# Two PSUM drains moved behind a branch, and earlier transposes of w3 with fewer load slots, in a one-core attention and mixture-of-experts kernel

## The chip, the cores and the metric

The kernel runs on one core of one Trainium2 chip. The metric is the device time of one launch in microseconds: the span from the first to the last instruction on the engines, and the little that lies around it. Three timed runs of the kernel before gave 1210.71, 1212.91 and 1214.0 us; their median is 1212.91 us. One more execution was taken with the profiler, and all rows below come from it.

## What is computed

Attention with a softmax over the features of q and over the sequence of k, then a mixture of eight experts with top-1 routing, then a bilinear network whose last two matrices follow each other without anything between them:

```python
def _moe_ref(x, modality_id, w_gate, modality_bias, w1, w2):
    ...
    for e in range(E):
        mask = e_idx == e
        h = np.maximum(x[mask] @ w1[e], 0.0)
        out[mask] = gate_w[mask, None] * (h @ w2[e])

def _moe2_ref(x, w1, w2, w3, w_out):
    a = x @ w1
    b = x @ w2
    h = a * b @ w3
    return h @ w_out
```

There are 4608 tokens of 512 features, 8 experts with 1024 hidden features, and in the last network w3 of 1024 by 1024 and w_out of 1024 by 512. All is float32 and stays that exact: an operand is split into a rounded part (hi) and the rest (lo), and each product is three matmuls (hi by hi, hi by lo, lo by hi).

## The kernel before

Attention comes first. Then the tokens, sorted by expert, go through ten **slots**: nine of 512 tokens and one of 256. A slot (the function `slot`, in parts that its argument names) loads the expert's W1 and W2 and gathers its tokens (part "l"), splits W1 on ScalarE and VectorE and transposes the tokens on TensorE (part "s"), multiplies by W1 in eight pieces m = 0 to 7 of 128 hidden features (part "a"; L752), each drained by a ReLU on ScalarE (L756) and a subtraction on VectorE (L757), and multiplies by W2 in four pieces (part "b"; L772), each drained by ScalarE (L775). The eight pieces of the W1 product take turns in PSUM banks 0, 1 and 2; the W2 product uses banks 3 and 4, the transposes of the tokens (L735) banks 5 and 7.

How many slots the experts need is known on the chip only. Behind part "a" of the **fourth slot** (n = D0 = 3) every engine loads the number `need` (L895), compares it and branches (L896). The body of the branch, with further slots, is for unlucky routings and does not run here. At the join each engine waits for its own semaphore and then adds to it what the body would have added, so that waits behind the join hold on both ways. Part "b" of the fourth slot stands behind the join.

After the slots comes a **stage of preparation** for the last network. w3 and w_out depend on no token, so they are multiplied with each other first, in eight blocks fb: `turned` loads 128 rows of w3, transposes them on TensorE into banks 5 and 7 (L978, four transposes for each half z) and splits each half on ScalarE (L966, out of PSUM) and VectorE (L967); `product` multiplies a block by the split w_out (L991, twelve matmuls for a half) into bank 3 or 4, which ScalarE drains (L994). In the same stage `factors` makes the operands of the last multiplication, a scheme of seven products in place of eight: four blocks, each of two loads, four sums on GpSimd (L1016) and seven splits on ScalarE (L1024) and VectorE (L1025). That multiplication (`quarter`, L1098) follows as soon as its token operands, loaded by `positions` (L1071), are split.

The loads of w_out, w3 and of the two factor matrices (their names in the rows are wo_f, w_f and m_f) go through five slots of 1024 floats in the tile `ca`, taken in turn (`ring`, `stage`; L959 and L961). The transposed and split halves of w3 live in four places (`th`): two for even blocks in `al` and `thm`, two for odd blocks in `tt`, which takes the place of the W2 product's output tile `yo`.

The order of all this on each engine is set by a planner (class `Plan`): every step has an engine, a cost, the keys that it reads and writes, and a rank, which is its place in the program plus `pri`; among the steps that can start, an engine takes the one of lowest rank. There is one plan ahead of the branch and one behind it. Semaphores are then set from the memory that instructions touch.

Of the kernel before, what the change touches and what calls it, by code (L numbers as in the profile page):

```python
# [142 lines left out]
def body(tc, q, k, v, mod, wgate, mbias, w1, w2, m1, m2, w3, wo, out):  # L143
# [529 lines left out]
    def slot(P, n, after=(), parts="lsab", T=None, again=False):  # L673
# [47 lines left out]
        if "s" in parts:  # L721
# [3 lines left out]
            for h in hs:  # L725
                for kp in range(2):
# [13 lines left out]
                    P.add("V", vt_(512), lambda hi=hi, lo=lo, p=p: V.tensor_tensor(lo(), p, hi().bitcast(F32), op=ALU.subtract), r=[K("bk", pb), K("xh", h, kp)], w=[K("xl", h, kp, "t")] + ([K("opened")] if n == 0 else []), pri=-230)  # L740

        if "a" in parts:
            for m in range(8):
                pb = m % 3
                p = lambda pb=pb: bank[pb][:, 0:N]
                ms = slice(128 * m, 128 * m + 128)

                for kk in range(4):

                    def mm(p=p, ms=ms, kk=kk):  # L750
                        for c, (i, z) in enumerate(PAIRS):
                            PE.matmul(p(), lhsT=W1(i)[:, TURN[kk], ms], rhs=XT(z)[:, kk, cols], start=(kk == 0 and c == 0), stop=(kk == 3 and c == 2))  # L752

                    P.add("P", 3 * one, mm, r=[K(x, TURN[kk] + 4 * (m // 4)) for x in ("w1h", "w1l")] + [K("xh", h, kk // 2) for h in hs] + [K("xl", h, kk // 2, "t") for h in hs] + ["Mb"], w=[K("bk", pb)])
                hh, hl = (lambda m=m: HT(0)[:, m, cols]), (lambda m=m: HT(1)[:, m, cols])
                P.add("S", ps_(N), lambda hh=hh, p=p: SC.activation(hh(), p(), AF.Relu), r=[K("bk", pb), "Mb"], w=[K("hh", h, m) for h in hs])  # L756
                P.add("V", vt_(N), lambda hh=hh, hl=hl, p=p: V.scalar_tensor_tensor(out=hl(), in0=p(), scalar=0.0, in1=hh().bitcast(F32), op0=ALU.max, op1=ALU.subtract),  # L757
                      r=[K("bk", pb)] + [K("hh", h, m) for h in hs], w=[K("hl", h, m) for h in hs])
            for f in range(8):
                split("w2", f, lambda f=f: M["w2r"][:, f], lambda f=f: W2(0)[:, f], lambda f=f: W2(1)[:, f], "Mb")  # L760

        if "b" in parts:
# [144 lines left out]
    for n in range(D0, X0):  # L907
        if n < D0 + 2:
            slot(P, n, parts="b" if n == D0 else "sab", T=aheads[n - D0])
        else:  # L910
            slot(P, n)
        units += 2 if n < F0 else 1
        while done < nj and done < NJ + (nj - NJ) * units // (2 * ND + NF - 1):
            doubles(done, *jobs[done])
            done += 1
# [25 lines left out]
    old = [K(x, i) for x in ("w1h", "w1l", "w2h", "w2l") for i in range(8)] + [K(x, b, i) for x in ("hh", "hl") for b in range(2) for i in range(8)]  # L941
    old += [K("xh", b, i) for b in range(2) for i in range(2)] + [K("xl", b, i, "t") for b in range(2) for i in range(2)]
    hand_over(old, two("Mf", 4))
    hand_over([K(x, i) for x in ("st", "T", "Q", "O") for i in range(2)] + [K("xg", b, i) for b in range(2) for i in range(2)], two("ring", 5) + two("tmp", 4) + two("ev", 2))
# [5 lines left out]
    def th(i, q, g=0, n=4):  # L950
        t, a = (("al", 8192), ("thm", 0), ("tt", 0), ("tt", 1024))[q]
        a += 512 * i + 128 * g
        return flat(M[t][:, a : a + 128 * n], n)

    def stage(nm, r):

        t, kk = ring[rot("ring", 5)]
        if nm == "wo":
# [4 lines left out]

    def split(src, sk, hi, lo, hk, lk, n, psum=False):

        P.add("S", (ps_ if psum else sb_)(n), lambda: SC.copy(hi(), src), r=sk, w=[hk])  # L966
        P.add("V", vt_(n), lambda: V.tensor_tensor(lo(), src, hi().bitcast(F32), op=ALU.subtract), r=list(sk) + [hk], w=[lk])  # L967

    def turned(fb):
        t, kk = stage("w3", fb)  # L970
        p2 = fb % 2
        for z in range(2):
# [6 lines left out]

            P.add("P", 0.43, tr, r=kk, w=[K("bk", pb)])  # L980
            q = 2 * p2 + z
            split(flat(bank[pb], 4), [K("bk", pb)], lambda q=q: th(0, q), lambda q=q: th(1, q), K("th", q), K("tl", q), 512, True)

    def product(fb):
        p2, pb = fb % 2, 3 + fb % 2
        for z in range(2):

            def mm(z=z):
                for g in range(4):
                    for n, (i, y) in enumerate(PAIRS):  # L990
                        PE.matmul(bank[pb], lhsT=th(i, 2 * p2 + z, g, 1)[:, 0], rhs=WO(y, 4 * z + g), start=(z == 0 and g == 0 and n == 0), stop=(z == 1 and g == 3 and n == 2))  # L991

            P.add("P", 2.73, mm, r=[K(x, 2 * p2 + z) for x in ("th", "tl")] + [K(x, g) for g in range(4 * z, 4 * z + 4) for x in ("wo", "wol")], w=[K("bk", pb)])
        P.add("S", ps_(512), lambda: SC.copy(evict[p2], bank[pb]), r=[K("bk", pb)], w=[K("ev", p2)])  # L994
# [32 lines left out]
    for r in range(4):  # L1027
        t, kk = stage("wo", r)
        for g in range(2):
            z = 2 * r + g  # L1030
            split(t[:, 512 * g : 512 * g + 512], kk, lambda z=z: WO(0, z), lambda z=z: WO(1, z), K("wo", z), K("wol", z), 512)
    turned(0)
    for fb in range(8):
        if fb < 7:
            turned(fb + 1)
        product(fb)
        if fb < 4:
            factors(fb // 2, fb % 2)


    t, kk = ring[rot("ring", 5)]
    oraw, orow = t[0:36, 0:256], t[0:36, 512:640]
# [243 lines left out]
```

## Time and profile before

| what | us |
|---|---|
| median of three timed runs | 1212.91 |
| the profiled execution, its own time | 1208.95 |
| its span, first to last instruction | 1207.2 |
| TensorE (PE) busy | 1130.9 |
| VectorE (DVE) busy | 859.3 |
| GpSimd (POOL) busy | 538.7 |
| ScalarE (ACT) busy | 526.3 |

The profiled execution lies 3.96 us below the median of the timed runs, and 1.75 us of its time lie outside the span. TensorE is the busiest engine by far, so the profile is read for what ends its idle times. A busy share says how long an engine had an instruction, not that it ran at its peak; the clock that TensorE was granted has a column of its own. PEld is TensorE's loading of weights, which overlaps its matmuls; a name with q (PEldq, DVEq) is an engine's instruction queue, where waits, loads of registers and branches stand.

### The profile page before, as it was taken

What the parts mean: (1) busy time and instruction counts of PE and PEld (TensorE: products, weight loads), DVE (VectorE), ACT (ScalarE), POOL (GpSimd) and SP (SyncE); (2) the same over time, 40 slices, a digit from 0 to 9 for tenths busy, and PEclk for the clock granted to TensorE, in tenths of its full rate; (3) what the DMA queues carried; (4) which work ended last, traced back from release to release, by engine and by line L of the source; (5) the groups of instructions that cost most, each with busy time, mean ns of one, the idle gap of its engine ahead of it and who ended that gap; (6) DMA issues with size and microseconds to landing.
All of it is one profiled execution on the core that took longest, in us unless ns stands there. A gap on an engine that the chain in (4) does not pass through costs nothing.

```text
span 1207.2 us, 22895 instructions
## 1 busy us (share of the span) xinstructions
PE 1130.9 (94%) x8605; PEld 1029.5 (85%) x8605; DVE 859.3 (71%) x1441; ACT 526.3 (44%) x1003; POOL 538.7 (45%) x538
## 2 busy tenths in 40 slices
PE   4777889999899999999999999999999999999996
PEld 3566768788788888888977999999999999999995
DVE  7979887997577787877594766656575689765550
ACT  3546455345344534533563232424232445655550
POOL 0445248853233333342260556454555576443332
PEclk9868789999999999999999999999999999999998
DMA  9982577773276467373673343434343438987741
GB/s 354 390 315 92 162 207 169 147 284 118 90 226 182 128 210 210 102 245 138 212 225 109 105 122 118 138 103 137 117 120 118 127 104 279 345 250 234 236 141 47
DMA packets 156140, 216.00 MB, mean 179 GB/s; under 512 B 19791, under 2 KB 90995, under 8 KB 156019
## 3 DMA queue, kind: packets, MB, share of 16 engines
q1 hardware_dynamic: 148946, 195.00, 50.8%
q0 software_dynamic: 7072, 19.44, 5.6%
q8 instruction: 69, 1.13, 0.4%
q14 instruction: 53, 0.43, 0.1%
HBM read 156.35 MB, written 74.82 MB: 191 GB/s over the span
## 4 chain that ended last, share of the span: by engine, by line
PE 67%; DVE 3%; issue 1%; DMA 1%; ACT 0%; POOL 0%; SPq 0%; DVEq 0%; POOLq 0%; ACTq 0%
PE pb L1098 29%; PE pb L1231 13%; PE pb L772 12%; PE pb L752 10%; PE pb L991 2%; DVE ar L1025 2%; PE pb L735 1%; DMA ca<-p_dram 0%; DMA p_dram<-ca 0%; DVE ar L967 0%; PE pb L978 0%; POOL out_dram L1205 0%; DVE tt L967 0%; DVE al L967 0%; DVE ca L1121 0%
## 5 line engine op out<-in xcount | busy, mean ns | idle before, releaser
L1098 PE MATMUL pb<-al,ar 128*128 128x384 f32 x1728 | 308.5, 336 | 1.1 <-ACT sx L1104 0.8
L1098 PEld LDWEIGHTS pb<-al,ar 128*128 128x128 f32 x1728 | 301.1, 188 | 1.6 <-ACT sx L1104 1.1
L772 PE MATMUL pb<-ar 128*128 128x512 f32 (+1 forms) x960 | 213.8, 381 | 0.0
L752 PE MATMUL pb<-ar 128*128 128x512 f32 (+1 forms) x960 | 212.5, 381 | 0.2 <-DVE ar L757 0.2
L752 PEld LDWEIGHTS pb<-ar 128*128 128x128 f32 x960 | 173.9, 189 | 34.3 <-DVE ar L757 0.6
L772 PEld LDWEIGHTS pb<-ar 128*128 128x128 f32 x960 | 173.2, 189 | 33.0
L1231 PE MATMUL pb<-ar 128*128 128x256 f32 x1512 | 182.8, 283 | 2.2 <-ACT ar L966 1.1
L1231 PEld LDWEIGHTS pb<-ar 128*128 128x128 f32 x1512 | 181.8, 192 | 3.2 <-ACT ar L966 1.3
L967 DVE TENSOR_TENSOR ar<-ca,ar 128x512 fp32r<-128x512 f32 x140 | 107.4, 776 | 54.6 <-ACT ar L966 52.7
L966 ACT CAST ar<-ca 128x512 fp32r<-128x512 f32 x140 | 86.0, 622 | 46.9 <-DMA ca<-p_dram 14.5
L756 ACT ACTIVATE ar<-pb 128x512 fp32r<-128x512 f32 (+1 forms) x80 | 46.2, 578 | 112.0 <-PE pb L752 111.9
L802 POOL TENSOR_TENSOR ca<-ca 128x512 f32<-128x512 f32 x40 | 56.4, 1415 | 79.9 <-DVE ca L801 72.1
L1104 ACT COPY sx<-pb 128x384 f32<-128x384 f32 x96 | 46.1, 482 | 90.5 <-PE pb L1098 63.9
L757 DVE SCALAR_TENSOR_TENSOR ar<-pb,ar 128x512 fp32r<-128x512 f32 (+1 forms) x80 | 52.7, 659 | 37.9 <-ACT ar L756 37.8
L330 POOL TENSOR_TENSOR kt<-kt,kr 128x384 f32<-128x384 f32 x36 | 45.2, 1294 | 75.0 <-ACT kr L324 60.0
L1132 POOL TENSOR_TENSOR ca<-ca 128x384 f32<-128x384 f32 x48 | 53.5, 1114 | 46.9 <-DVE ca L1132 46.9
L1107 POOL TENSOR_TENSOR ca<-ca,sx 128x384 f32<-128x384 f32 x24 | 27.3, 1139 | 95.3 <-ACT sx L1104 95.3
L775 ACT COPY yo<-pb 128x512 f32<-128x512 f32 (+1 forms) x40 | 22.6, 566 | 107.2 <-PE pb L772 97.3
L688 DVE TENSOR_TENSOR ar<-w2r,ar 128x512 fp32r<-128x512 f32 x60 | 46.2, 796 | 28.0 <-ACT ar L686 27.0
L1104 ACT COPY ca<-pb 128x384 f32<-128x384 f32 x48 | 23.0, 481 | 87.1 <-PE pb L1098 82.3
L688 POOL TENSOR_TENSOR ar<-w2r,ar 128x512 fp32r<-128x512 f32 x20 | 28.2, 1411 | 69.2 <-ACT ar L686 69.1
L1098 PE MATMUL pb<-thm,ar 128*128 128x384 f32 x288 | 59.0, 340 | 0.0
(282 smaller groups left out, 1781.3 us busy)
## 6 DMA issues: line engine op xcount, KB each, us to landing
p_dram<-ca SPq DMA_DIRECT2D x168, 192.0 KB, 2.3
ca<-p_dram SPq DMA_DIRECT2D x126, 256.0 KB, 3.8
w1r<-in_moe_w_dram SPq DMA_DIRECT2D x10, 2048.0 KB, 7.8
w2r<-in_moe_w_dram SPq DMA_DIRECT2D x10, 2048.0 KB, 9.5
ca<-in_moe_w_dram SPq DMA_DIRECT2D x32, 512.0 KB, 4.1
kt<-in_k_dram SPq DMA_DIRECT2D x8, 1152.0 KB, 10.8
qt<-in_q_dram SPq DMA_DIRECT2D x8, 1152.0 KB, 13.2
vt<-in_v_dram SPq DMA_DIRECT2D x8, 1152.0 KB, 16.2
```

What stands on the lines that cost most here:

```text
L688: P.add(g, c, lambda: e.tensor_tensor(lo(), raw(), hi().bitcast(F32), op=ALU.subtract), r=[K(nm + "r", i), K(nm + "h", i), extra], w=[K(nm ...
L752: PE.matmul(p(), lhsT=W1(i)[:, TURN[kk], ms], rhs=XT(z)[:, kk, cols], start=(kk == 0 and c == 0), stop=(kk == 3 and c == 2))
L756: P.add("S", ps_(N), lambda hh=hh, p=p: SC.activation(hh(), p(), AF.Relu), r=[K("bk", pb), "Mb"], w=[K("hh", h, m) for h in hs])
L757: P.add("V", vt_(N), lambda hh=hh, hl=hl, p=p: V.scalar_tensor_tensor(out=hl(), in0=p(), scalar=0.0, in1=hh().bitcast(F32), op0=ALU.max, o ...
L772: PE.matmul(p(), lhsT=W2(i)[:, f, ns], rhs=HT(y)[:, f, cols], start=(f == 0 and c == 0), stop=(f == 7 and c == 2))
L802: P.add("G", gt_(512), lambda: G.tensor_tensor(Tf, Tf, Qf, op=ALU.add), r=[K("Q", b)], w=[K("T", b)])
L966: P.add("S", (ps_ if psum else sb_)(n), lambda: SC.copy(hi(), src), r=sk, w=[hk])
L967: P.add("V", vt_(n), lambda: V.tensor_tensor(lo(), src, hi().bitcast(F32), op=ALU.subtract), r=list(sk) + [hk], w=[lk])
L1098: PE.matmul(bk(j), lhsT=Mt[:, f, a, i, m, t], rhs=X(y, x)[:, t], start=(fresh and t == 0 and n == 0), stop=(t == 1 and n == 2), skip_group ...
L1104: P.add("S", ps_(HB), lambda j=j, to=to: SC.copy(S(to), bk(j)), r=[bkk(j)], w=[sk(to)])
L1132: P.add(eng, c(HB), lambda: e.tensor_tensor(t[:, sl], x, y, op=op), r=kk, w=[k_])
L1231: PE.matmul(bk(j), lhsT=At[z][:, m, i, f], rhs=Bt[:, x, y, f], start=(fresh and f == 0 and n == 0), stop=(f == 3 and n == 2), skip_group_c ...
```

## The change

Three things are edited. First, the drains of pieces 6 and 7 of the fourth slot's W1 product (a ReLU and a subtraction each) are taken out of part "a", which stands ahead of the branch, into a part "z" that the plan behind the branch begins with. The matmuls stay where they are. Second, the loads of w3 get two slots of the ring for themselves, and w_out and the factors the other three. Third, the transposes of w3 and their splits get a lower rank (`pri` of -120, and -400 for block 0), and block 1 puts its two halves into `ar`, into memory that the W1 halves of the slots held and that the factors of the second matrix take later.

```diff
+        def leave(m):
+            pb = m % 3
+            p = lambda pb=pb: bank[pb][:, 0:N]
+            hh, hl = (lambda m=m: HT(0)[:, m, cols]), (lambda m=m: HT(1)[:, m, cols])
+            P.add("S", ps_(N), lambda hh=hh, p=p: SC.activation(hh(), p(), AF.Relu), r=[K("bk", pb), "Mb"], w=[K("hh", h, m) for h in hs])
+            P.add("V", vt_(N), lambda hh=hh, hl=hl, p=p: V.scalar_tensor_tensor(out=hl(), in0=p(), scalar=0.0, in1=hh().bitcast(F32), op0=ALU.max, op1=ALU.subtract),
+                  r=[K("bk", pb)] + [K("hh", h, m) for h in hs], w=[K("hl", h, m) for h in hs])
...
+                if n != D0 or m < 6:
+                    leave(m)
...
+        if "z" in parts:
+            for m in (6, 7):
+                leave(m)
...
-            slot(P, n, parts="b" if n == D0 else "sab", T=aheads[n - D0])
+            slot(P, n, parts="zb" if n == D0 else "sab", T=aheads[n - D0])
...
+    hand_over(old[:16], [K(x, i) for x in ("th", "tl") for i in (4, 5)])
...
-        t, a = (("al", 8192), ("thm", 0), ("tt", 0), ("tt", 1024))[q]
+        t, a = (("al", 8192), ("thm", 0), ("tt", 0), ("tt", 1024), ("ar", 3584), ("ar", 4608))[q]
...
-        t, kk = ring[rot("ring", 5)]
+        t, kk = ring[3 + rot("w3", 2) if nm == "w3" else rot("ring", 3)]
...
+    quarter_of = lambda fb, z: 4 + z if fb == 1 else 2 * (fb % 2) + z
+
-    def turned(fb):
+    def turned(fb, ahead=-120):
...
-            P.add("P", 0.43, tr, r=kk, w=[K("bk", pb)])
-            q = 2 * p2 + z
-            split(flat(bank[pb], 4), [K("bk", pb)], lambda q=q: th(0, q), lambda q=q: th(1, q), K("th", q), K("tl", q), 512, True)
+            P.add("P", 0.43, tr, r=kk, w=[K("bk", pb)], pri=ahead)
+            q = quarter_of(fb, z)
+            split(flat(bank[pb], 4), [K("bk", pb)], lambda q=q: th(0, q), lambda q=q: th(1, q), K("th", q), K("tl", q), 512, True, ahead)
...
-    turned(0)
+    turned(0, -400)
...
+        if fb == 1:
+            hand_over([K(x, i) for x in ("th", "tl") for i in (4, 5)] + two("Mf", 4), [])
```

Where it moves instructions is shown by the order of the two built programs. VectorE before the change, the last rows ahead of the branch (L757 is a subtraction; pb_2296, pb_2297 and pb_2298 are banks 0, 1 and 2):

```order
L757 SCALAR_TENSOR_TENSOR ar<-pb_2298,ar 128x512
L757 SCALAR_TENSOR_TENSOR ar<-pb_2296,ar 128x512
L757 SCALAR_TENSOR_TENSOR ar<-pb_2297,ar 128x512
L757 SCALAR_TENSOR_TENSOR ar<-pb_2298,ar 128x512
L757 SCALAR_TENSOR_TENSOR ar<-pb_2296,ar 128x512
L757 SCALAR_TENSOR_TENSOR ar<-pb_2297,ar 128x512
L895 TENSOR_LOAD need
L896 COMPARE_AND_BRANCH
```

VectorE with the change, the first rows behind the join (L747 is the same subtraction, L740 the split of the transposed tokens out of banks 5 and 7):

```order
L906 UNCONDITIONAL_BRANCH x2
L747 SCALAR_TENSOR_TENSOR ar<-pb_2296,ar 128x512
L747 SCALAR_TENSOR_TENSOR ar<-pb_2297,ar 128x512
L740 TENSOR_TENSOR ar<-pb_76,ar 128x2x256
L740 TENSOR_TENSOR ar<-pb_78,ar 128x2x256
L688 TENSOR_TENSOR ar<-w1r,ar 128x512 x3
```

The two last subtractions of the fourth slot stand behind the join instead of ahead of the branch; ScalarE's two ReLUs moved in the same way. TensorE before the change, from the last slot's W2 product (L772) into the stage of preparation (L978 transposes, L991 products):

```order
L772 MATMUL pb_2299<-ar 128x256 x24
L772 MATMUL pb_75<-ar 128x256 x24
L772 MATMUL pb_2299<-ar 128x256 x24
L772 MATMUL pb_75<-ar 128x256 x24
L978 MATMUL pb_76<-ident,ca 128x128 x4
L978 MATMUL pb_78<-ident,ca 128x128 x4
L978 MATMUL pb_76<-ident,ca 128x128 x4
L991 MATMUL pb_2299<-al 128x512 x12
L978 MATMUL pb_78<-ident,ca 128x128 x4
L991 MATMUL pb_2299<-al,thm 128x512 x12
```

TensorE with the change, the same place (L782 is the W2 product, L991 are now the transposes):

```order
L782 MATMUL pb_2299<-ar 128x256 x12
L991 MATMUL pb_76<-ident,ca 128x128 x4
L991 MATMUL pb_78<-ident,ca 128x128 x4
L782 MATMUL pb_2299<-ar 128x256 x12
L782 MATMUL pb_75<-ar 128x256 x3
L991 MATMUL pb_76<-ident,ca 128x128 x4
L782 MATMUL pb_75<-ar 128x256 x3
L991 MATMUL pb_78<-ident,ca 128x128 x4
L782 MATMUL pb_75<-ar 128x256 x18
L991 MATMUL pb_76<-ident,ca 128x128 x4
L991 MATMUL pb_78<-ident,ca 128x128 x4
L782 MATMUL pb_2299<-ar 128x256 x24
```

The transposes of blocks 0, 1 and 2 stand among the matmuls of the last W2 product; behind it, products come at once.

## Rows read from the trace of the kernel before

**Rows 1.** The chain that ended last: start us, length us, what.
```profile
328.92 3.41 PE pb L772 x12
332.32 0.87 PE pb L735 x8
333.20 19.09 PE pb L772 x84
...
589.69 11.53 PE pb L772 x96
...
657.18 1.05 PE pb L1098 x6
```

**Rows 2.** Stretches: length, busy PE, PEld, DVE, ACT, POOL, PEclk, DMA share, GB/s.
```profile
326.90:330.10 3.20, 3.12 (x12) 2.86 (x13) 2.38 (x4) 2.83 (x6) 0.00 (x0) 0.50 0.19 5
330.20:333.60 3.40, 3.40 (x20) 2.88 (x20) 2.92 (x5) 2.26 (x5) 1.36 (x1) 1.00 0.07 1
```

**Rows 3.** Timeline around the branch: start us, length us, engine, line, what [idle before].
```profile
317.37 0.60 ACT L756 ACTIVATE ar<-pb 128x512 fp32r<-128x512 f32 x1 [2.40 <-PE pb L752]
318.00 0.69 DVE L757 SCALAR_TENSOR_TENSOR ar<-pb,ar 128x512 fp32r<-128x512 f32 x1 [2.31 <-ACT ar L756]
322.47 0.60 ACT L756 ACTIVATE ar<-pb 128x512 fp32r<-128x512 f32 x1 [2.06 <-PE pb L752]
323.10 0.69 DVE L757 SCALAR_TENSOR_TENSOR ar<-pb,ar 128x512 fp32r<-128x512 f32 x1 [1.96 <-ACT ar L756]
326.98 1.94 PE L735 MATMUL pb<-ident,ca 128*128 128x128 f32 x8 [4.54 <-DVEq L896]
```

**Rows 4.** Line 896, the branch: durations (ns min/median/max), first and last start us.
```profile
L896 PEldq COMPARE_BRANCH  x1: 3732/3732/3732, 318.8 to 318.8; - x1
L896 PEldq EVENT_SEMAPHORE  x1: 51/51/51, 322.6 to 322.6; - x1
L896 ACTq EVENT_SEMAPHORE  x1: 17/17/17, 325.9 to 325.9; - x1
L896 DVEq EVENT_SEMAPHORE  x1: 21/21/21, 326.8 to 326.8; - x1
```

**Rows 5.** The columns of rows 2: the last W2 product, then the stage of preparation.
```profile
589.70:601.20 11.50, 11.50 (x98) 11.50 (x98) 3.13 (x6) 3.53 (x8) 3.92 (x4) 1.00 0.62 217
601.20:657.00 55.80, 52.28 (x257) 42.39 (x255) 38.07 (x46) 28.73 (x53) 20.03 (x13) 1.00 0.55 175
```

**Rows 6.** TensorE's waits from 601.3 to 657 us: total, times, longest.
```profile
PE pb L978 <- DVE al L967: 1.5, 1, 1.5
PE pb L978 <- DVE tt L967: 1.0, 1, 1.0
PE pb L991 <- DVE al L967: 1.0, 1, 1.0
```

**Rows 7.** ScalarE's timeline, splits of w_out during the last slot.
```profile
590.20 0.62 ACT L966 CAST al<-ca 128x512 fp32r<-128x512 f32 x1 [1.01 <-DMA ca<-wo_f]
...
591.00 1.65 ACT L966 CAST al<-ca 128x512 fp32r<-128x512 f32 x3
```

**Rows 8.** Lines 1025 and 967 by form: durations (ns min/median/max), first and last start.
```profile
L1025 DVE TENSOR_TENSOR ar<-ca,ar x28: 676/681/1790, 602.2 to 637.0; 128x512 fp32r<-128x512 f32 x28
L967 DVE TENSOR_TENSOR tt<-pb,tt x8: 674/680/692, 606.7 to 647.0; 128x512 fp32r<-128x512 f32 x8
```

**Rows 9.** Timeline of GpSimd and VectorE, second and last block of factors.
```profile
611.23 5.94 POOL L1016 TENSOR_TENSOR ca<-ca 128x512 f32<-128x512 f32 x4 [8.88 <-DMA ca<-m_f]
...
632.57 5.07 DVE L1025 TENSOR_TENSOR ar<-ca,ar 128x512 fp32r<-128x512 f32 x7
```

**Rows 10.** Lines 961 and 1071, loads: time from issue to landing.
```profile
DMA to landing us min/median/max: 4.1/4.9/9.4
DMA to landing us min/median/max: 3.7/4.7/5.6
```

**Rows 11.** Groups of instructions from 601.2 to 657 us: busy us, mean ns | idle before.
```profile
L1025 DVE TENSOR_TENSOR ar<-ca,ar 128x512 fp32r<-128x512 f32 x28 | 27.6, 1036 | 8.2 <-ACT ar L1024 8.2
```

More of the change, by code (lines that the diff above doesn't have):

```diff
@@ L754, in slot @@
                     P.add("P", 3 * one, mm, r=[K(x, TURN[kk] + 4 * (m // 4)) for x in ("w1h", "w1l")] + [K("xh", h, kk // 2) for h in hs] + [K("xl", h, kk // 2, "t") for h in hs] + ["Mb"], w=[K("bk", pb)])
[L755 to L758, printed above, removed]
+                if n != D0 or m < 6:
+                    leave(m)
             for f in range(8):
                 split("w2", f, lambda f=f: M["w2r"][:, f], lambda f=f: W2(0)[:, f], lambda f=f: W2(1)[:, f], "Mb")
+        if "z" in parts:
+            for m in (6, 7):
+                leave(m)
         if "b" in parts:
@@ L962, in stage, with split @@
         return t, kk
-    def split(src, sk, hi, lo, hk, lk, n, psum=False):
-        P.add("S", (ps_ if psum else sb_)(n), lambda: SC.copy(hi(), src), r=sk, w=[hk])
-        P.add("V", vt_(n), lambda: V.tensor_tensor(lo(), src, hi().bitcast(F32), op=ALU.subtract), r=list(sk) + [hk], w=[lk])
-    def turned(fb):
+    def split(src, sk, hi, lo, hk, lk, n, psum=False, pri=0):
+        P.add("S", (ps_ if psum else sb_)(n), lambda: SC.copy(hi(), src), r=sk, w=[hk], pri=pri)
+        P.add("V", vt_(n), lambda: V.tensor_tensor(lo(), src, hi().bitcast(F32), op=ALU.subtract), r=list(sk) + [hk], w=[lk], pri=pri)
+    quarter_of = lambda fb, z: 4 + z if fb == 1 else 2 * (fb % 2) + z
+    def turned(fb, ahead=-120):
         t, kk = stage("w3", fb)
@@ L990, in mm @@
                     for n, (i, y) in enumerate(PAIRS):
-                        PE.matmul(bank[pb], lhsT=th(i, 2 * p2 + z, g, 1)[:, 0], rhs=WO(y, 4 * z + g), start=(z == 0 and g == 0 and n == 0), stop=(z == 1 and g == 3 and n == 2))
-            P.add("P", 2.73, mm, r=[K(x, 2 * p2 + z) for x in ("th", "tl")] + [K(x, g) for g in range(4 * z, 4 * z + 4) for x in ("wo", "wol")], w=[K("bk", pb)])
+                        PE.matmul(bank[pb], lhsT=th(i, quarter_of(fb, z), g, 1)[:, 0], rhs=WO(y, 4 * z + g), start=(z == 0 and g == 0 and n == 0), stop=(z == 1 and g == 3 and n == 2))
+            P.add("P", 2.73, mm, r=[K(x, quarter_of(fb, z)) for x in ("th", "tl")] + [K(x, g) for g in range(4 * z, 4 * z + 4) for x in ("wo", "wol")], w=[K("bk", pb)])
         P.add("S", ps_(512), lambda: SC.copy(evict[p2], bank[pb]), r=[K("bk", pb)], w=[K("ev", p2)])
@@ L1036, in body @@
         product(fb)
+        if fb == 1:
+            hand_over([K(x, i) for x in ("th", "tl") for i in (4, 5)] + two("Mf", 4), [])
         if fb < 4:
             factors(fb // 2, fb % 2)
-    t, kk = ring[rot("ring", 5)]
+    t, kk = ring[rot("ring", 3)]
     oraw, orow = t[0:36, 0:256], t[0:36, 512:640]
```

## The prediction, made before the change was run

> **What bounds the kernel now.** I read the page first: TensorE is busy 1130.9 us of a span of 1207.2, and no other engine comes near, so what counts is where TensorE stands still or runs at a lower clock. The chain of waits comes next. At the two places that the change touches it runs on TensorE itself: W2 product and transposes behind the branch, the last slot's W2 product, and the start of the last multiplication at 657.18 [rows 1]. So a microsecond saved on TensorE there comes off the end, unless something else becomes late.
>
> The third view is the stretches, with the granted clock. From 326.9 to 330.1 TensorE was granted 0.50, the lower of its two levels (1.2 GHz of 2.4); from 330.2 it has 1.00 again [rows 2]. What it did before: nothing for 4.54 us. The timeline shows that the eight transposes of L735 at 326.98 waited that long for VectorE's queue at the branch [rows 3]. The fourth view, the branch's own rows, tells why. TensorE's queue compares at 318.8 and is through the join at 322.6, while its last matmuls still run. ScalarE and VectorE come through the join at 325.9 and 326.8 only [rows 4], because each first drains piece 7: a ReLU starts at 322.47, a subtraction at 323.10 [rows 3], and only then do they load the number and branch. TensorE sits through that, since its transposes wait for counts that these joins add.
>
> The second place is the stage of preparation, 601.2 to 657.0. TensorE is busy 52.28 of 55.80 us: 3.52 us idle, at full clock [rows 5]. The waits of that stretch are three, all on VectorE's subtraction for the low half of a w3 block [rows 6].
>
> **The change, part by part.** *The drains.* Nothing is added or removed: two ReLUs (0.60 us) and two subtractions (0.69 us) move behind the join. Now the last instruction ahead of ScalarE's branch is the ReLU of piece 5, at 317.37, and ahead of VectorE's the subtraction at 318.00 [rows 3]. From the start of the last drain to the join I read 325.9 - 322.47 = 3.4 us on ScalarE and 326.8 - 323.10 = 3.7 us on VectorE. So ScalarE should join at 320.8 and VectorE at 321.7, both ahead of TensorE's own join at 322.63. From VectorE's join to the first transpose were 0.2 us; TensorE then starts again at about 322.8, in place of 326.98: **A = 4.2 us**. Bounds: the whole idle time, 4.5, from above. From below 1.6, if TensorE cannot have its branch behind it while matmuls run (a rival, below). A loss is excluded: no engine reaches its join later than before.
>
> What is late next? The drained pieces 6 and 7 are operands of the W2 product. Piece 6 drains after the joins (ReLU to 321.4, subtraction to 322.4), piece 7 as before, when its matmuls end: to 323.8. TensorE wants piece 6 after its transposes (0.87) and 18 matmuls; 84 of these took 19.09 us, 0.227 each [rows 1], so at 322.8 + 0.87 + 4.1 = 327.8. That hides both drains with 4 us to spare; without that cover they would cost 2.6 us. Behind them on VectorE stand the splits of the transposed tokens. They wait for TensorE's transposes, which end at 323.7, as long as the drains. The drains have no DMA, and neither SP's nor GpSimd's queue is passed.
>
> *The clock.* Behind 0.4 us of idle time I expect the full clock. For it: in the stage of preparation single waits of 1.5 us [rows 6] left it at 1.00 [rows 5]. At 0.50 the eight transposes took 1.94 us against 0.87 for the same eight at 332.32, and the twelve matmuls 3.41 against 12 x 0.227 = 2.73 [rows 1, 3]: **B = 1.07 + 0.68 = 1.75 us**. Bounds: nothing and 1.75.
>
> *The transposes and the ring.* The transposes of blocks 0 to 2 (24 matmuls) now stand among the last slot's W2 product, and products follow it at once. TensorE has no less work; what can go are the 3.52 us of waits. The transposes get there before TensorE is out of work if block 0 has landed. It is now the fourth load in the queue. TensorE wants it twelve matmuls into the product: 96 took 11.53 us [rows 1], so at 589.69 + 12 x 0.12 = 591.13. Before, the third load (w_out) was awaited until 590.20, and the fourth fed the run of three splits from 591.00, whose last two start no later than 591.55 [rows 7]. So the fourth load landed between 590.2 and 591.55, and TensorE waits 0 to 0.4 us. I take the worse end: **C = 3.52 - 0.4 = 3.1 us**; bounds 0 (a wait on the splits remains, a rival) and 3.5. The six moved halves cost ScalarE 6 x 0.6 and VectorE 6 x 0.68 [rows 8] in the 11.5 us from 589.7, where these are busy 3.53 and 3.13 [rows 5]: 7.1 and 7.2 of 11.5, so the W2 product's own drains still find room.
>
> What pays is the factors, which now have three slots of the ring in place of five, and lower rank. Their last splits end at 632.57 + 5.07 = 637.64 [rows 9]. GpSimd waited 8.88 us for the second block's loads [rows 9]; with three slots each of three blocks may wait for a landing, 4.9 us [rows 10]: 14.7 in place of 8.9, and the factors end 5.8 later, at 643.4. Behind them come a load of tokens (4.7, [rows 10]) and its split (1.9, at half as wide again as the 0.60 and 0.68 of a half block): 650.0. The multiplication can start at 657.0 - 3.1 = 653.9 on this time axis, so 4 us of slack stay, and I cost it at nothing.
>
> **Sum:** 4.2 + 1.75 + 3.1 = 9.05 us off the profiled execution's 1208.95, that is 1199.9. That execution lies 3.96 below the median, so the time is **1203.9 us**.
>
> **The rivals.** *The low halves stay late (0.20).* In the new order, runs of up to five factor splits stand ahead of a w3 subtraction on VectorE. They should take 0.68 us but range up to 1.79, mean 1.036 [rows 8, 11]; five cost 5.2 us in place of 3.4. If the subtractions queue behind them, waits like the three of now come back at other blocks: C = 0, 1212.91 - 5.95 = 1207.0. For it: that spread is there on splits with both operands in SBUF, while the subtraction out of PSUM always takes 0.67 to 0.69 [rows 8]. Against: blocks 0 to 2 are now ahead by three blocks.
>
> By the Trainium skill ("SBUF — State Buffer", Terms), VectorE and GpSimd share one pair of SBUF ports, held for a whole instruction while the loser fully blocks. By that rule the splits would stretch wherever GpSimd's sums run, and the spread of the splits agrees with it; which sum held which split these rows do not show.
>
> *The clock falls anyway (0.06).* Any pause at the branch might bring 0.50; B = 0, 1212.91 - 7.3 = 1205.6. Against it the waits of 1.5 us at 1.00.
>
> *TensorE pays its branch late (0.06).* If its compare could only run once its matmuls have ended, 2.9 us (ScalarE's and VectorE's time from the end of the last drain to the join) would follow 322.43: restart at 325.3, A = 1.6, and the clock cold, B = 0: 4.7 us, 1208.2. Against it: TensorE's queue compared at 318.8 [rows 4], and that does not change.
>
> By the Trainium skill ("Runtime: NRT & Kernel Launch", Instruction fetch mechanics) a taken branch outside the fetched pages makes the engine fetch the target page before it goes on. By that rule each engine pays this from its own branch on, which puts the gain where the branch is reached early; the 3.7 us of TensorE's compare beside running matmuls agrees.
>
> *The ring starves the factors (0.05, the slower side).* Three slots hold one block's two loads and half the next, so a load waits for GpSimd to free a slot, and SP's queue, in which w3 loads stand between, holds later ones. If each of three landings costs the largest 9.4 us, and 4.1 (the shortest) behind a w3 load [rows 10], the factors end at 637.6 - 8.9 + 3 x 13.5 = 669.2, the multiplication can start 6.6 (tokens and split) later, at 675.8, 21.9 behind 653.9: 1203.9 + 21.9 = 1225.8. It decides once the factors end behind 653.9 - 6.6 = 647.3, and makes the kernel slower than before from 656.4 on (9.05 later). For it: the 8.88 us wait is there already with five slots. Against: the median landing is 4.9.
>
> *The change does nothing (0.02):* another engine (SP or GpSimd) keeps the join at 326.8 and the waits move: 1212.9.
>
> **How the numbers follow.** The forecast keeps 0.61. A measurement tells about 0.3%, 3.6 us, from no change, so faster means below 1209.3. That holds for the forecast, the late halves, the clock and half of the late branch (it lies 1.1 us inside): 0.61 + 0.20 + 0.06 + 0.03 = 0.90. The same: the other half and nothing done, 0.05. Slower: the starved ring, 0.05. Low end: upper bounds 4.5 + 1.75 + 3.5 give 1203.2, less the 2.2 us by which the lowest run lies under its median: 1201.0. High end: the late halves' 1207.0 plus the 1.1 us by which the highest run lies above, which is the late branch's 1208.2 too.
>
> **What would show it.** Right: before L735's first transposes behind the branch under 0.5 us of idle time, not released by VectorE's queue; full clock from 322 to 330; these eight in 0.87 us. In the stage of preparation idle time near 0.4, no waits on w3's subtractions, the factors done before 647.3 - 5.95 = 641.3, and the last multiplication starting near 648. Wrong: VectorE's or ScalarE's join still last at the branch; a wait of TensorE for pieces 6 or 7; GpSimd waiting for landings by more than 15 us in all; or TensorE waiting for factors or token splits ahead of the last multiplication.

## The result, and the profile after

Six timed runs of the changed kernel have a median of 1200.93 us (1199.88 to 1207.11), six of the kernel before 1213.26 us. The ratio is 0.9915, with a 95% interval of 0.9889 to 0.9942: 7 to 13.5 us less. The forecast of 1203.9 is a ratio of 0.9926 to the median it started from, and its range of 1201.0 to 1208.2 one of 0.9902 to 0.9961. The changed kernel is faster, by about as much as forecast. (The two medians lie 12.3 us apart, more than the ratio says, and the lower one is 0.1 us below the low end of the range in microseconds.)

The profiled execution took 1204.72 us (span 1203.0), only 4.2 less than the one before. Followed along TensorE, the difference falls into five pieces. "Branch" is here from the end of TensorE's last W1 matmul ahead of the branch to the start of the long W2 run behind it, and "stage" from the start of the last slot's W2 product to the first matmul of the last multiplication; both are read at the starts of instructions in the two timelines.

| piece, us | before | after | forecast of the difference |
|---|---|---|---|
| start to the last W1 matmul ahead of the branch | 322.44 | 325.80 (+3.36) | none |
| branch | 10.52 | 5.55 (-4.97) | -5.95 |
| from there to the last W2 product | 256.57 | 256.52 | none |
| stage | 67.50 | 64.36 (-3.14) | -3.1 |
| last multiplication and the rest | 550.20 | 550.76 (+0.56) | none |

So the change took off 8.1 us in this pair of executions, and 3.4 came back ahead of anything that it touches. All fourteen profiles of this study show that piece anywhere between 321.9 and 331.0 us, while the middle piece is 256.5 to 256.6 in all but one (257.3 in e8, below). Some of the scatter lies ahead of the first W1 matmul, which starts between 157.3 and 161.6 us, and more behind it: 162.3 to 169.4 us from there to the last W1 matmul ahead of the branch. That is why the experiments below are compared by branch and stage, and by the ratio of the timed runs.

TensorE's timeline at the branch after, with the drains (columns as in [rows 3]):

```profile
320.73 0.60 ACT L746 ACTIVATE ar<-pb 128x512 fp32r<-128x512 f32 x1 [2.40 <-PE pb L760]
321.36 0.69 DVE L747 SCALAR_TENSOR_TENSOR ar<-pb,ar 128x512 fp32r<-128x512 f32 x1 [2.31 <-ACT ar L746]
326.75 1.08 ACT L746 ACTIVATE ar<-pb 128x512 fp32r<-128x512 f32 x2 [5.42 <-PEq L906]
326.87 1.06 PE L735 MATMUL pb<-ident,ca 128*128 128x128 f32 x8 [1.07 <-PEq L906]
327.38 1.29 DVE L747 SCALAR_TENSOR_TENSOR ar<-pb,ar 128x512 fp32r<-128x512 f32 x2 [5.32 <-ACT ar L746]
```

The branch's own rows (as [rows 4]):

```profile
L906 PEldq COMPARE_BRANCH  x1: 4372/4372/4372, 322.2 to 322.2; - x1
L906 DVEq EVENT_SEMAPHORE  x1: 21/21/21, 325.1 to 325.1; - x1
L906 ACTq EVENT_SEMAPHORE  x1: 17/17/17, 325.2 to 325.2; - x1
L906 PEldq EVENT_SEMAPHORE  x1: 51/51/51, 326.6 to 326.6; - x1
```

VectorE and ScalarE now come through the join at 325.1 and 325.2, ahead of the end of TensorE's last matmul (325.80). The join that everybody waits for is TensorE's own, at 326.6. The idle time before the transposes went from 4.54 to 1.07 us. The chain and the clock behind it, against [rows 1, 2]:

```profile
326.87 1.06 PE pb L735 x8
327.93 2.78 PE pb L782 x12
```

```profile
326.90:330.10 3.20, 3.20 (x19) 2.76 (x20) 2.72 (x5) 3.20 (x7) 0.00 (x0) 1.00 0.15 9
587.87:652.23 64.36, 63.39 (x354) 54.19 (x353) 35.27 (x52) 31.57 (x61) 21.63 (x16) 1.00 0.57 191
```

The first of these two stretches has the full clock where there was 0.50; the second is the whole stage, with TensorE idle for 0.97 us. Its waits, and what became of the factors (as [rows 6, 11]; GpSimd's row begins at 603 us, behind the first block's three first sums and the wait ahead of them, VectorE's is the whole stage):

```profile
PE pb L991 <- DMA ca<-w_f: 1.0, 2, 0.8
```

```profile
L1029 POOL TENSOR_TENSOR ca<-ca 128x512 f32<-128x512 f32 x13 | 17.8, 1392 | 19.8 <-DMA ca<-m_f 13.3 <-DVE ar L1038 6.2
```

```profile
L1038 DVE TENSOR_TENSOR ar<-ca,ar 128x512 fp32r<-128x512 f32 x28 | 21.1, 807 | 11.8 <-ACT ar L1037 11.8
```

No wait on a w3 subtraction is left; the two that remain are for w3's loads, 0.17 and 0.80. Behind the first block GpSimd waits longer for its loads (13.3 us against 8.9 [rows 9]), and the splits of the factors on VectorE have become shorter: a mean of 0.807 us in place of 1.036 [rows 11].

### The profile page after: what moved, and what is told of

Its sections match the earlier page's. It is cut to its first block, busy times and chain, and to the rows that moved or that the text cites. A ratio compares the mean times of both kernels' runs of the same rounds, so it can differ in the third digit from the quotient of the medians.

```text
span 1203.0 us, 22890 instructions
## 1 busy us (share of the span) xinstructions
PE 1127.9 (94%) x8605; PEld 1025.8 (85%) x8605; DVE 855.5 (71%) x1441; ACT 525.6 (44%) x1003; POOL 534.8 (44%) x538
## 4 chain that ended last, share of the span: by engine, by line
PE 68%; DMA 2%; DVE 0%; issue 0%; SPq 0%; ACT 0%; POOL 0%; POOLq 0%; ACTq 0%; DVEq 0%
PE pb L1113 29%; PE pb L1246 13%; PE pb L782 11%; PE pb L760 9%; PE pb L1004 4%; DMA ca<-w_f 1%; PE pb L735 1%; DMA p_dram<-ca 1%; PE pb L991 1%; DMA ca<-p_dram 0%; DVE ar L978 0%; SPq L970 0%; POOL out_dram L1220 0%; SPq L1209 0%; DVE ca L1089 0%
## 5 line engine op out<-in xcount | busy, mean ns | idle before, releaser
L782 PE MATMUL pb<-ar 128*128 128x512 f32 (+1 forms) x960 | 214.0, 381 | 0.0
L782 PEld LDWEIGHTS pb<-ar 128*128 128x128 f32 x960 | 172.8, 188 | 32.8
L1246 PE MATMUL pb<-ar 128*128 128x256 f32 x1512 | 182.9, 283 | 2.8 <-ACT ar L977 1.6
L1246 PEld LDWEIGHTS pb<-ar 128*128 128x128 f32 x1512 | 181.8, 192 | 3.8 <-ACT ar L977 1.8
L978 DVE TENSOR_TENSOR ar<-ca,ar 128x512 fp32r<-128x512 f32 x140 | 107.8, 779 | 54.3 <-ACT ar L977 50.7
L747 DVE SCALAR_TENSOR_TENSOR ar<-pb,ar 128x512 fp32r<-128x512 f32 (+1 forms) x80 | 52.6, 659 | 39.1 <-ACT ar L746 37.9
L715 POOL DMA_INDIRECT ca<-x_dram,ord x38 | 38.3, 1008 | 45.5 <-DVE ord L622 20.6
```

Of the source, the lines that this page charges most:

```text
L782: PE.matmul(p(), lhsT=W2(i)[:, f, ns], rhs=HT(y)[:, f, cols], start=(f == 0 and c == 0), stop=(f == 7 and c == 2))
L1246: PE.matmul(bk(j), lhsT=At[z][:, m, i, f], rhs=Bt[:, x, y, f], start=(fresh and f == 0 and n == 0), stop=(f == 3 and n == 2), skip_group_c ...
```

## The experiments

Three questions were open: do the parts add up, what sets TensorE's restart at the branch, and which of the stage's three edits (ring, ranks, place in `ar`) carries its 3 us. In this table "beside" counts the factor splits, of 28, that overlap one of GpSimd's sums in time.

| kernel | ratio of times, 95% | idle at the branch | branch | stage | beside |
|---|---|---|---|---|---|
| before | 1 | 4.54 | 10.52 | 67.50 | 16 |
| whole change | 0.9915 (0.9889-0.9942) | 1.07 | 5.55 | 64.36 | 5 |
| e1 drains only | 0.9960 (0.9938-0.9981) | 0.42 | 4.89 | 67.49 | 15 |
| e2 stage only | 0.9957 (0.9937-0.9976) | 4.40 | 10.99 | 63.39 | 4 |
| e3 three behind | 0.9917 (0.9888-0.9947) | 0.62 | 5.09 | 63.21 | 4 |
| e4 one behind | 0.9922 (0.9894-0.9951) | 1.70 | 6.38 | 63.38 | 5 |
| e5 drains, ranks | 1.0001 (0.9981-1.0021) | 0.53 | 4.99 | 74.85 | 14 |
| e6 drains, ring, place | 0.9950 (0.9924-0.9975) | 0.46 | 4.93 | 65.03 | 5 |
| e7 drains, ranks, place | 0.9963 (0.9942-0.9984) | 0.55 | 5.01 | 68.24 | 15 |
| e8 ring of 3 and 2 | 0.9953 (0.9932-0.9974) | 0.36 | 4.83 | 69.55 | 9 |
| e9 drains, ring | 0.9944 (0.9926-0.9962) | 0.54 | 5.01 | 65.84 | 12 |
| e10 drains, ring, ranks | 0.9968 (0.9952-0.9983) | 0.76 | 5.22 | 67.19 | 10 |
| e11 e5, sums on VectorE | 0.9949 (0.9929-0.9968) | 0.44 | 4.90 | 65.46 | none |
| e12 e1, sums on VectorE | 0.9948 (0.9928-0.9968) | 0.42 | 4.90 | 65.98 | none |

### Do the two parts add up? (e1, e2)

e1 puts `leave` and the part "z" into the kernel before and nothing else. e2 is the whole change with

```diff
-                if n != D0 or m < 6:
+                if True:
                     leave(m)
...
-        if "z" in parts:
-            for m in (6, 7):
-                leave(m)
...
-            slot(P, n, parts="zb" if n == D0 else "sab", T=aheads[n - D0])
+            slot(P, n, parts="b" if n == D0 else "sab", T=aheads[n - D0])
```

> The kernel before with nothing but the drains of pieces 6 and 7 moved behind the join. Both theories below measure the branch from the end of TensorE's last W1 matmul ahead of it to the end of the second eight transposes (start of the long W2 run): 10.77 us before, 5.56 us with the whole change. Theory (the parts add up): branch 5.6 us, stage of preparation (start of the last W2 product to the first matmul of the last multiplication) 67.5 us as before, time 5 us under before. Rival (the microseconds won at the branch are given back, because the loads of the next slot now come too late): a new wait of TensorE between the branch and the last slot, time within 1 us of before. On the branch itself: TensorE idle 1.07 us if three engines that fetch behind their branches at the same time slow each other (compare row of TensorE 4.4 us), about 0.2 to 0.4 if the 1.07 was chance.

> The whole change but with the drains of pieces 6 and 7 ahead of the branch again. Theory (the parts add up): branch 10.8 us as before with the granted clock 0.50 behind it, stage 64.4 us, time 3.1 us under before. Rival (the stage wins only because the branch part shifts it against the loads): stage 66 us or more, time under 1.5 us better than before. TensorE's compare row 3.7 us if it is slowed only by other engines' branches at the same time.

(The 10.77 us in these texts was read at the end of the second transposes, the 5.56 at the start of the matmuls behind them. Read alike they are 10.52 and 5.55.)

e1: branch 4.89, stage 67.49, no new wait up to the last slot; 0.4% faster. e2: branch 10.99 with the clock at 0.50, stage 63.39; 0.43% faster. Together that is the 0.85% of the whole change: the parts add up, and neither rival holds. The stage alone gives 4.1 us, more than the 3.1 in the profile of the whole change, because e2 waited only 0.18 us for w3's loads. e3 and e4 have no such wait either. The 0.80 us wait for the third load is in one profile of four with this ring, these ranks and this place. That load was issued 2.7 to 2.9 us behind the start of the stage in all four, so it is the landing that scatters.

### What sets TensorE's restart? (e3, e4)

The two kernels differ from the whole change in which pieces are left for behind the join:

```diff
-                if n != D0 or m < 6:
+                if n != D0 or m < 5:
...
-            for m in (6, 7):
+            for m in (5, 6, 7):
```

and, in e4, `m < 7` and `(7,)`.

> The whole change, with the drain of piece 5 behind the join too. ScalarE and VectorE then branch 2.7 to 3.6 us earlier. Theory A (TensorE's way through the branch was lengthened from 3.7 to 4.4 us because ScalarE, VectorE and TensorE fetch at the same time): their fetches are over sooner, TensorE's compare row goes back to about 3.7, it joins 0.2 us behind its last matmul, idle 0.3, branch 4.9 us, time 0.7 us under the whole change. Theory B (TensorE needs 0.8 to 1.1 us behind its last matmul or weight load in any case, which VectorE's late join hid before): compare 4.4, idle 1.07, branch 5.6, time the same.

> The whole change, with the drain of piece 7 alone behind the join. ScalarE and VectorE branch 2.4 us later than with two. Theory: VectorE's join is last again, 3.7 us behind the start of piece 6's subtraction, which puts the restart 1.9 us behind the last matmul; branch 1.3 to 1.5 us longer than with two behind at full clock; with the clock at 0.50 after 1.9 us of idle time 1.75 more. Theory A of the three-behind run: TensorE is alone when it compares, its compare row is 3.7 us. Theory B: 4.4 us.

In e3 TensorE's compare row was 3.93 us, with ScalarE and VectorE 3.2 us and more ahead; in e1, with all three close together as in the whole change, it was 3.73. So branches close together are not what lengthened TensorE's: Theory A falls. Theory B falls too, with idle times of 0.36 to 0.76 us in all ten experiments with two or three pieces behind. TensorE compares 3.6 us ahead of its last matmul's end and joins 3.7 to 4.4 us after that, so its join lands 0.1 to 0.8 us behind the matmuls. The 1.07 us of the whole change is the longest of eleven. (ScalarE takes 3.8 to 4.2 us from compare to join where TensorE compares 0.9 us behind it, 2.6 to 2.9 where TensorE compared 1.6 us or more ahead of it, and 3.5 in e3, where TensorE follows 3.6 us later; it is early enough in all of them with two or three pieces behind. The cause was not tried.)

e4, VectorE's join last again:

```profile
323.62 1.06 PE L735 MATMUL pb<-ident,ca 128*128 128x128 f32 x8 [1.70 <-DVEq L906]
```

```profile
321.90:323.60 1.70, 0.03 (x1) 0.01 (x1) 0.00 (x0) 0.00 (x0) 0.00 (x0) 1.00 0.06 15
323.70:326.00 2.30, 2.30 (x15) 2.03 (x16) 0.65 (x2) 1.28 (x3) 0.00 (x0) 1.00 0.24 10
```

1.70 us idle (1.9 expected) and the clock stays at 1.00. Even one piece left for behind the join takes most of the gain at the branch, the clock's part with it; the timed ratios of two, three and one cannot be told apart.

### Ranks, ring and place (e5, e6, e7, e9, e10)

Each kernel has the drains behind the join. e5 takes the ring and the place out again, e6 only the ranks, e7 only the ring. e9 keeps only the ring of the three, e10 keeps ring and ranks. The place without ring and ranks was not run.

```diff
-        t, kk = ring[3 + rot("w3", 2) if nm == "w3" else rot("ring", 3)]
+        t, kk = ring[rot("ring", 5)]
...
-    quarter_of = lambda fb, z: 4 + z if fb == 1 else 2 * (fb % 2) + z
+    quarter_of = lambda fb, z: 2 * (fb % 2) + z
...
-    def turned(fb, ahead=-120):
+    def turned(fb, ahead=0):
...
-    turned(0, -400)
+    turned(0)
```

The first pair of lines is in e5 and e7, the second in e5, e9 and e10, the last two in e6 and e9.

> The whole change, but the loads go through the old ring of five slots in turn and block 1 keeps its old place: only the ranks (and the drains) are left. The stage, from the start of the last W2 product to the first matmul of the last multiplication, was 67.5 us before and 63.2 to 64.4 with the whole change. Theory (the ranks carry the gain, because they put the first transposes ahead of the end of the W2 product): stage under 65 us. Rival (without slots of its own a w3 load comes after those of the factors, and without the place in ar block 2 waits for block 0's product): waits of TensorE for w3's load or for a subtraction come back, stage 66 us or more.

> The whole change, but transposes of w3 and their splits keep their old rank; ring and the place in ar as changed. TensorE's order in the stage is then that of before, with all transposes behind the W2 product. Theory: three waits on the subtractions stay, stage 67 us or more; the factors end later than before, by up to 6 us, still without a wait for them. Rival (the loads were what counted): stage under 65 us.

> The whole change, but with one ring of five slots for all loads; ranks and the place in ar as changed. Theory (the ranks and the place carry it, the split of the ring only says which load goes first): stage 63 to 65 us, with single waits of up to 1 us for w3's load. Rival (the split of the ring carries it): stage 66 us or more, with waits for w3 behind factor loads. The factors, with five slots to take, end sooner than with three.

> The drains behind the join and the split of the ring (two slots for w3, three for the rest), and nothing else: old ranks, block 1 in its old place. With the place in ar as well the stage took 65.0 us, with the drains alone 67.5. Theory (three slots hold the factor loads back, so GpSimd's sums no longer run beside VectorE's splits of factors): stage 65 to 66 us, at most 8 of the 28 splits beside a sum, their mean under 0.9 us. Rival (the place in ar did it, since block 1's splits no longer wait for a place): stage 67 us or more.

> The whole change without the place in ar for block 1. Theory (the ring carries the stage and the ranks take away what waits are left): stage under 64.5 us, like the whole change (63.2 to 64.4). Rival (without the place the transposes of block 2 have nowhere to go, as with the ranks alone): waits of 1 us or more of TensorE on a subtraction, stage 65.5 us or more.

The theory that the ranks carry the gain fell at once. Without ring and place they make the stage 7.35 us longer. TensorE's and VectorE's timelines in e5:

```profile
611.24 1.11 PE L991 MATMUL pb<-ident,ca 128*128 128x128 f32 x4 [3.65 <-DVE tt L978]
612.00 5.17 PE L1004 MATMUL pb<-al,tt 128*128 128x512 f32 x12
...
636.47 1.65 PE L991 MATMUL pb<-ident,ca 128*128 128x128 f32 x8 [3.17 <-DVE al L978]
```

```profile
603.00 7.57 DVE L1038 TENSOR_TENSOR ar<-ca,ar 128x512 fp32r<-128x512 f32 x7 [8.95 <-ACT ar L1037]
610.50 1.28 DVE L978 TENSOR_TENSOR tt<-pb,tt 128x512 fp32r<-128x512 f32 x2
...
622.60 13.21 DVE L1038 TENSOR_TENSOR ar<-ca,ar 128x512 fp32r<-128x512 f32 x9
635.74 0.68 DVE L978 TENSOR_TENSOR al<-pb,al 128x512 fp32r<-128x512 f32 x1
```

A run of seven factor splits, then one of nine that took 13.21 us, stands ahead of the subtraction that TensorE waits for; it stands idle 3.65 and 3.17 us. Behind each wait the clock is down, so that twelve matmuls of a product took 5.17 us in place of 2.9:

```profile
607.00:611.20 4.20, 0.58 (x3) 0.14 (x1) 4.20 (x5) 2.59 (x5) 3.50 (x3) 0.84 0.02 9
611.20:617.00 5.80, 5.76 (x16) 4.68 (x17) 4.27 (x7) 2.66 (x5) 0.51 (x1) 0.53 0.51 136
```

Ring and place without the ranks (e6) have TensorE's order of before and still a stage of 65.03: of the three waits only the first is left, which comes of the transposes standing behind the W2 product.

```profile
603.46 0.65 PE L991 MATMUL pb<-ident,ca 128*128 128x128 f32 x4 [1.44 <-DVE al L978]
```

The ranks take away just that wait, once ring and place are there: the stage goes from 65.03 to between 63.2 and 63.4. With one of the two missing it is longer: with the place but without the ring (e7) it is 68.24, more than with the drains alone (67.49), with runs of five, nine and six factor splits ahead of w3's subtractions; with the ring but without the place (e10) it is 67.19, worse than the ring alone (65.84). There three splits beside a sum took 4.49 us ahead of one subtraction, and TensorE waited 2.65:

```profile
625.20 4.49 DVE L1038 TENSOR_TENSOR ar<-ca,ar 128x512 fp32r<-128x512 f32 x3 [1.83 <-ACT ar L1037]
629.62 0.68 DVE L978 TENSOR_TENSOR tt<-pb,tt 128x512 fp32r<-128x512 f32 x1
```

So four of the five theories were wrong here: those of e5, e7 and e10 fell to the numbers of their rivals, and that of e6 to 65.03, just above what its rival had said. The reason that the rivals of e5 and e7 had in common, w3's loads behind those of the factors, is little of it: TensorE waited for w3's loads for 0.09 us in e5 and 0.79 in e7, and for splits of w3 for 6.8 and 2.9. e9's stage came out as expected, but not by what was expected of it: 12 of 28 splits ran beside a sum, at a mean of 1.047 us for all. By itself the ring does not keep sums and splits apart; only with the place do they fall to 5 (e6). Why they do was not pursued.

### The starved ring (e8)

```diff
-        t, kk = ring[3 + rot("w3", 2) if nm == "w3" else rot("ring", 3)]
+        t, kk = ring[2 + rot("w3", 3) if nm == "w3" else rot("ring", 2)]
```

> The whole change, but with three slots for w3 and two for w_out and the factors: the ring is starved one step further. Theory (the price of the smaller ring lies in the slack of the factors, which end 8.4 us ahead of the last multiplication now and need 6.6 of it): with two slots the four blocks of factors follow each other at 14 us or more in place of 11, and their first load is behind two more of w3; they end 10 us later or more, and the last multiplication, no longer TensorE's own, starts 5 to 15 us later: stage 69 us or more, time 4 to 10 us above the whole change. Rival (GpSimd's sums and the splits set the pace, not the landings): stage under 64 us, the wait for the third w3 load (0.8 us) gone.

The size came as the theory said, the way to it only in part. The stage is 69.55 us (70.34 with eight transposes of w3 that here stand ahead of the last W2 product), and the kernel by its ratio some 0.4% slower than the whole change, with intervals that overlap a little. GpSimd waits 39.9 us for loads, the first block's included, where the whole change, counted alike, has 32.1. The factors' last split ends at 657.54, 5.1 ahead of the last multiplication at 662.68:

```profile
L1029 POOL TENSOR_TENSOR ca<-ca 128x512 f32<-128x512 f32 x16 | 22.8, 1447 | 45.0 <-DMA ca<-m_f 39.9 <-DVE tt L978 4.8
```

```profile
656.85 0.69 DVE L1038 TENSOR_TENSOR ar<-ca,ar 128x512 fp32r<-128x512 f32 x1 [2.34 <-ACT ar L1037]
```

In the whole change they end 8.4 us ahead (652.23 less 643.83), and the split of the tokens that follows ends 2.9 us ahead:

```profile
643.15 0.68 DVE L1038 TENSOR_TENSOR ar<-ca,ar 128x512 fp32r<-128x512 f32 x1
648.40 0.96 DVE L978 TENSOR_TENSOR al<-ca,al 128x768 fp32r<-128x768 f32 x1 [4.57 <-ACT al L977]
```

Counted from the start of the last W2 product, e8's factors end about 8.5 us later than these (10 or more were expected) and its last multiplication starts 5.2 us later. But most of this is not the factors' lateness. TensorE's waits in e8, and what stood ahead of the longest:

```profile
PE pb L991 <- DVE al L978: 3.7, 2, 2.0
PE pb L1060 <- ACT ca L1007: 0.7, 1, 0.7
PE pb L1113 <- ACT al L977: 0.5, 1, 0.5
```

```profile
634.83 6.37 DVE L1038 TENSOR_TENSOR ar<-ca,ar 128x512 fp32r<-128x512 f32 x4 [0.31 <-ACT ar L1037]
641.13 0.68 DVE L978 TENSOR_TENSOR al<-pb,al 128x512 fp32r<-128x512 f32 x1
```

Of 4.93 us idle, 3.73 are waits for w3's subtractions behind runs of four factor splits (5.62 and 6.37 us) that overlap sums, as in e5. Only 1.20 us stand directly ahead of the last multiplication: 0.72 for the drain of the last product and 0.48 for the split of the tokens, which is late. Behind the second wait, of 2.03 us, the granted clock was 0.50, and TensorE's busy time in the stage is 2.0 us longer than in the whole change. So the prediction's rival of the starved ring is at work with one slot less, but for about a microsecond; the rest of the loss came by the path of another rival, the late halves.

### Splits against sums (e11, e12)

```diff
-            P.add("G", gt_(512), lambda: G.tensor_tensor(tmp[n], x, y, op=op), r=r, w=[K("tmp", n)])
+            P.add("V", vt_(512), lambda: V.tensor_tensor(tmp[n], x, y, op=op), r=r, w=[K("tmp", n)])
```

> The ranks-alone kernel (stage 74.85 us, 14 of 28 factor splits beside a sum of GpSimd at 1.46 us in place of 0.68, waits of TensorE of 3.7 and 3.2 us), with the sixteen sums computed on VectorE in place of GpSimd. Theory (its loss comes from splits and sums that hold each other up): all 28 splits at 0.68 us; VectorE has 16 x 0.69 = 11 us of sums more and 11 us of held splits less, the waits behind runs of splits get shorter, the clock stays at 1.00: stage 68 to 70 us. Rival (its loss comes from the order alone, seven and nine splits ahead of a w3 subtraction): waits of 3 us and more stay, stage 74 us or more.

> The drains-alone kernel (stage 67.5 us with three waits on w3's subtractions, 15 of 28 splits beside a sum at 1.35 us), with the sums on VectorE. Theory (the held splits make the low halves of w3 late): splits at 0.68 us, the waits shrink, stage 65 to 66.5 us. Rival (the first wait, 1.4 us, comes with the transposes standing behind the W2 product, and VectorE now has the sums too): stage 67 us or more.

In e11 all 28 splits take the short time (min, median, max in ns), where e5's range up to 1.844 us:

```profile
L1038 DVE TENSOR_TENSOR ar<-ca,ar x28: 680/684/693, 602.9 to 636.3; 128x512 fp32r<-128x512 f32 x28
```

e11's stage fell from 74.85 to 65.46 us, with 1.8 us of waits and full clock: more than expected, though VectorE now does eleven microseconds of sums besides. For e5's first long wait the holding is shown: the same run of seven splits stands ahead of the same two subtractions and takes 4.30 us in place of 7.57, and TensorE waits 0.75 us in place of 3.65. For the second it is not, because the planner gave VectorE's queue another order there: the run of nine splits is gone. So how much of the 9.4 us is the holding and the clock behind it, and how much the order, stays open. e12 does the same for the order of before, 67.49 to 65.98; its waits on w3, 1.4 and 1.1, are the first and one other. It gains 1.5 us with the old ring and place, where ring and place gain 2.5 with the sums on GpSimd (e6). Neither beats the whole change, whose stage TensorE already fills, and none of the twelve kernels shows a lower ratio.

## Why the prediction was right, and where it was not

*Where the drains go.* Right in the mechanism: VectorE's and ScalarE's joins moved ahead of TensorE's last matmul. A was forecast at 4.2 us; the profile gives 4.54 - 1.07 = 3.47, and the other kernels with two or three pieces behind 3.8 to 4.2. The step that failed in this one execution is "TensorE's own join at 322.63" (0.2 behind its last matmul): here it came 0.8 behind, since its way through the branch took 4.4 us and not 3.7. It is not the rival "TensorE pays its branch late": the compare still ran 3.6 us ahead of the last matmul's end, and what is left uncovered is 0.1 to 0.8 us, not 2.9.

*What is late next.* The slack was right, the way to it not. The text had piece 6 drained at once after ScalarE's join. In fact ScalarE's ReLU waits for TensorE's join (5.42 us, PEq L906), because the count that it waits for includes what TensorE adds there. Both drains run from 326.75 to 328.67, and TensorE wants them six matmuls into the run that starts at 331.35, at 332.7. Four microseconds of cover, as forecast.

*The clock.* Right: 1.00 behind a pause of 1.07. The term was 1.75; the two rows are now 1.06 and 2.78 in place of 1.94 and 3.41 [rows 1, 3], 1.51 us. The term was over-sized because it priced the first eight transposes by a row of eight that run straight behind other matmuls (0.87).

*The stage.* C was 3.1, and 3.14 in the profile, but made up otherwise than forecast, and by chance that low. Block 0 was awaited for 0.17 (0 to 0.4 forecast) and the third load for 0.80, which was not in the sum; without such a wait the stage is 63.2 to 63.4, a gain of 4.1 to 4.3. Beyond the 3.52 us of idle time, this is 0.6 us of busy time (63.97 us in the stage before, 63.39 after): the row behind a wait is longer too, as before the change eight transposes behind one took 1.25 us and eight without one 1.04.

The reasoning of the step failed. It put the gain down to the transposes standing early and treated ring and place as costs. The ranks without the other two cost 7.35 us; ring and place give 2.5 of the gain, and the ranks the other 1.7 upon them.

*The late halves.* The rival had its mechanism right and its condition wrong: long runs of factor splits held by sums do stand ahead of w3's subtractions as soon as ring or place are missing, and with another split of the ring (e8). Its bottom price, C = 0, was too mild: e5 gives C = -7.35, and its clock falls with it.

*The factors.* They end at 643.83, which on the axis of before (the last W2 product started at 589.53, now at 587.87) is 645.5: 2.1 later than forecast, 1.8 ahead of 647.3. Behind the first block GpSimd waited 13.3 us for landings where 14.7 were forecast, but for two blocks and not for three; ahead of the second block it waited 6.2 us for VectorE's splits, which the forecast did not have.

*The sum.* 9.05 us forecast, 8.1 by branch and stage in one profile, about 9.7 by e1's branch and e2's stage, 10.3 by the ratio of the timed runs.

## What to carry to other kernels

Ahead of a branch that every engine must pass, leave for behind the join what the slower engines would drain last: the busiest engine then waits for its own way through the branch only, and the gain includes the clock that a long pause costs. Where a planner orders the queues, price a change of ranks by the runs of other work that it lets stand ahead of the awaited instruction, and try each edit without the others: here an edit that costs 7 us without two others took off the last wait once they were there. Read a stage in its own anchors, since the scatter of an earlier one (9 us here) is as large as the gain.

## What the runs showed of the hardware

**Splits and sums.** A VectorE split with both operands in SBUF took 0.67 to 0.69 us in every case where no GpSimd sum overlapped it, and up to 1.85 beside one (mean 1.30 for the 16 of the kernel before). GpSimd's sums took 1.27 to 1.30 us where no split overlapped them, and beside splits 1.46 to 1.64 on average over a kernel, 1.81 at most. The subtraction out of PSUM took 0.67 to 0.69 beside the sums too. e5's two queues show the turns: its sums

```profile
628.90 6.37 POOL L1029 TENSOR_TENSOR ca<-ca 128x512 f32<-128x512 f32 x4 [1.60 <-DVE ar L1038]
```

ran at 1.3 to 1.7 us each while VectorE's splits took 1.74 to 1.78. The Trainium skill ("SBUF — State Buffer", Terms) says of the port pair that the two engines share that it is held for the whole instruction and the loser fully blocks; e11 and e12, without sums on GpSimd, agree with it.

**The clock.** Pauses of TensorE of 0.4 to 1.7 us at the branch and of 2.65 in e10's stage left the granted clock at 1.00. Behind pauses of 3.17 and 3.65 (e5) it averaged 0.70 and 0.53 over the next 5.6 and 5.8 us, and behind 4.40 (e2) and 4.54 (before) it was 0.50 for about 3 us. But a pause of 2.03 in e8's stage was followed by 0.50 too (642.5 to 645.0 us), and late in the kernel (matmuls of L1246), behind 84 matmuls that ran for 10.3 us, a pause of 1.57 in e7 was followed by 0.61 over 4 us and one of 1.59 in the whole change by 1.00. So in these runs the length of a pause alone does not tell which of the two levels follows it; what does was not tried.

**The branch.** From compare to join, in fourteen profiles: TensorE 3.7 to 4.4 us beside running matmuls; ScalarE 2.6 to 2.9 in the three with one or no piece behind, and 3.5 to 4.2 in the eleven with two or three; VectorE 2.9 to 3.3, but 5.2 in e3; GpSimd 1.2; SyncE 2.5 to 2.8. From the start of its last drain to its join ScalarE took 4.5 us in the whole change (320.73 to 325.2) where 3.4 was forecast. The reason was not tried.
